# Groups 1 to 3 of a first feed-forward layer by Strassen's scheme too, and its successor's operands made a block ahead and kept on chip

## The chip, the cores and the metric

The kernel runs on one core of a Trainium2 chip. The metric is the device time of one execution in microseconds (us), lower is better. A core has five engines with a queue each: PE (TensorE, the matrix unit), DVE (VectorE), ACT (ScalarE), POOL (GpSimd) and SP (SyncE, which here only issues DMAs; ACT and POOL issue some too). Each engine works off its own list of instructions in order; semaphores make one wait for another.

## The reference, cut to what matters

Linear attention over 4 batches, 8 heads, 576 tokens and 64 columns a head gives x of 2304 tokens x 512 columns; then two feed-forward layers (FFN 1 and FFN 2) of 512 to 2048 to 512 columns.

```python
q_p, k_p = phi(q), phi(k)                     # random features, 128 per head
kv = np.einsum('bhsm,bhsd->bhmd', k_p, v)
x = (einsum(q_p, kv) / einsum(q_p, z))        # -> (2304, 512)
h = x @ w_in ; r = np.maximum(h, 0.0) ; y = (r * r) @ w_out          # FFN 1
h = y @ w2_in ; out = np.where(h > 0, h, exp(min(h, 0)) - 1) @ w2_out # FFN 2
```

All of it is float32. The FFN weights come as 64-bit floats and are turned into 32-bit ones on the chip.

## The kernel before, in words

**Limbs.** Each float32 operand of a matmul is held as two tiles, a high limb (names with h: xh, wh, gh) and a low limb (xl, wl, gl). A product is three matmuls: high x high, high x low, low x high. ACT makes high limbs (a copy), DVE low ones (`minus`, a subtraction).

**Blocks, tiles, groups.** The tokens lie in five blocks: blocks 0 to 3 have 512 tokens (one batch each), block 4, called B, has the 256 left over. The 2048 hidden columns are 16 tiles f of 128, in four groups g of four. Names carry these numbers: `st1_3_1` is the staged weight of layer 1 (FFN 2; FFN 1 is 0), tile 3, w_out (0 is w_in).

**FFN 1 before.** `steps` is the list of (group, block, tile): all five blocks for the four tiles of group 0, then of group 1, and so on. For each step `gemm1` (12 matmuls of 512 columns into one PSUM bank ph; ACT's relu r and square gh; DVE's gf and gl) is issued, then `gemm2` of the step two before (12 matmuls into py). After a group's four tiles DVE adds py into ya, the block's running sum. In group 0 blocks 0 to 2 go in halves of 256 tokens, the first 11 steps being woven into the attention; from step 11 on nothing else is left (`alone`). A `gemm1` also moves the decoding of weights ahead (`make`: ACT makes cm, DVE cv, of the staged tile st) and takes up to two entries of the list `later`.

**FFN 2 before.** `second` goes through tours, one for each group and block. A full block's tour is one of Strassen's products over the tiles: seven products (pa, pw, pb; 12 matmuls of 256 columns each) in place of eight, on sums of x pieces and on sums of weights (a, b, c, d; POOL makes them from each two tiles, cs and cd), and four chunks of the second matmul (12 matmuls of 512 columns). Copies us and vs and sums c21 and c22 join the products. Block B has no such scheme (pe, po: 24 matmuls each). x's operands of FFN 2 are made by `operands` at the end of each block of FFN 1 (POOL: eight subtractions of 256 columns; ACT and DVE split them) and stored to DRAM; each tour loads its own (`load_x`), only block 0's are kept on chip for the first.

**What sets the order.** The program is written out in order by hand. All tiles (x, limbs, weights, ya, temporaries) are pages of one pool of 93 (128x512 floats each): the next tile takes the page used longest ago, and its first writer waits for the last user of it. Eight PSUM banks go in the same way. Weights are fetched through three staging buffers, before the change by SP's queue, or POOL's for FFN 2 from tile 4 on.

## Time and profile before

| what | value |
|---|---|
| median of 3 runs | 938.9 us (938.43 to 938.97) |
| the profiled execution | 939.0 us, its span 937.2 us |
| granted TensorE clock, mean | 0.998 |
| PE busy | 921.5 us (98%) |
| DVE, ACT, POOL busy | 650.6, 498.7, 176.8 us |
| DMA | 131.25 MB, 140 GB/s over the span |

The span is the time from the first to the last instruction. PE's end times are modelled, so a busy PE need not be one at its peak.

### The profile page before, as it was taken

The numbers are of one execution on the slowest core, as the hardware profiler recorded it, in microseconds if no ns is written. First come the engines' busy times: TensorE is split into PE (matmuls) and PEld (weight loads), VectorE is DVE, ScalarE is ACT, GpSimd is POOL, SyncE is SP. The second block draws the span as 40 slices with busy tenths as digits, with TensorE's granted clock in tenths as the row PEclk, the third lists the DMA queues.
The fourth block names the chain that finished last, engine by engine and source line by source line (L and its number), as shares of the span: only waits on it lengthen the run. The fifth ranks groups of instructions, "written<-read, shape, count | busy, mean of one in ns | idle before, by whom it ended". The sixth has DMA issues, their size and how long they took to land.

```text
span 937.2 us, 17705 instructions
## 1 busy us (share of the span) xinstructions
PE 921.5 (98%) x6723; PEld 812.3 (87%) x6723; DVE 650.6 (69%) x1144; ACT 498.7 (53%) x1080; POOL 176.8 (19%) x299
## 2 busy tenths in 40 slices
PE   8998999999999999999999999999999999999997
PEld 7887889998888888888888888998898889988996
DVE  5989885753873378336789858996678667975553
ACT  6998975432432234223454446776377646665451
POOL 7666641000000000000133424400121002100000
PEclk9999999999999999999999999999999999999999
DMA  8554510110220023001254599785557756663632
GB/s 242 165 165 116 133 47 2 46 45 1 91 90 1 1 78 103 1 0 46 68 184 154 191 313 349 292 281 206 159 198 246 260 161 200 210 216 112 227 132 72
DMA packets 93749, 131.25 MB, mean 140 GB/s; under 512 B 30304, under 2 KB 48736, under 8 KB 93664
## 3 DMA queue, kind: packets, MB, share of 16 engines
q1 hardware_dynamic: 88240, 113.44, 37.2%
q0 software_dynamic: 4576, 16.26, 5.2%
q8 instruction: 53, 0.87, 0.4%
q10 hardware_dynamic: 848, 0.43, 0.2%
q14 instruction: 32, 0.26, 0.1%
HBM read 109.12 MB, written 20.97 MB: 139 GB/s over the span
## 4 chain that ended last, share of the span: by engine, by line
PE 87%; DVE 6%; ACT 5%; issue 1%; DMA 1%; SPq 0%; POOL 0%; ACTq 0%; DVEq 0%; POOLq 0%
PE py L688 21%; PE ph L498 21%; PE py L537 21%; PE pb L649 7%; PE pa L649 5%; PE pw L649 5%; PE po L769 1%; PE pe L769 1%; ACT ph0q L355 1%; DVE xl L76 1%; ACT ph2k L355 1%; ACT ph2q L355 1%; PE pn L419 1%; DVE cv L145 0%; ACT xh L453 0%
## 5 line engine op out<-in xcount | busy, mean ns | idle before, releaser
L509 ACT ACTIVATE r<-ph 128x512 f32<-128x512 f32 (+1 forms) x92 | 46.7, 507 | 229.3 <-PE ph L498 229.2
L513 DVE TENSOR_TENSOR gf<-r 128x512 f32<-128x512 f32 (+1 forms) x92 | 55.6, 605 | 130.3 <-ACT r L509 130.3
L498 PE MATMUL ph<-xh,wh 128*128 128x512 f32 (+1 forms) x368 | 127.5, 346 | 1.6 <-DVE xs L406 1.2
L537 PE MATMUL py<-gh,wh 128*128 128x512 f32 (+1 forms) x368 | 127.7, 347 | 0.0
L537 PE MATMUL py<-gl,wh 128*128 128x512 f32 (+1 forms) x368 | 126.9, 345 | 0.0
L537 PE MATMUL py<-gh,wl 128*128 128x512 f32 (+1 forms) x368 | 126.9, 345 | 0.0
L498 PE MATMUL ph<-xh,wl 128*128 128x512 f32 (+1 forms) x368 | 126.8, 345 | 0.0
L498 PE MATMUL ph<-xl,wh 128*128 128x512 f32 (+1 forms) x368 | 126.8, 345 | 0.0
L76 DVE TENSOR_TENSOR gl<-gf,gh 128x512 fp32r<-128x512 f32 (+1 forms) x164 | 106.2, 648 | 24.1 <-ACT gh L671 13.5
L688 PE MATMUL py<-wh,gh 128*128 128x512 f32 x288 | 113.6, 395 | 0.0
L688 PE MATMUL py<-wh,gl 128*128 128x512 f32 x288 | 113.6, 394 | 0.0
L688 PE MATMUL py<-wl,gh 128*128 128x512 f32 x288 | 113.4, 394 | 0.0
L662 DVE SCALAR_TENSOR_TENSOR r<-r,t 128x512 f32<-128x512 f32 x72 | 51.6, 716 | 67.0 <-ACT t L661 67.0
L498 PEld LDWEIGHTS ph<-xh,wh 128*128 128x128 f32 x368 | 69.2, 188 | 11.5 <-issue 1.3
L537 PEld LDWEIGHTS py<-gh,wh 128*128 128x128 f32 x368 | 69.2, 188 | 9.5
L537 PEld LDWEIGHTS py<-gh,wl 128*128 128x128 f32 x368 | 69.2, 188 | 9.2
L537 PEld LDWEIGHTS py<-gl,wh 128*128 128x128 f32 x368 | 69.2, 188 | 9.2
L498 PEld LDWEIGHTS ph<-xh,wl 128*128 128x128 f32 x368 | 69.2, 188 | 9.1
L498 PEld LDWEIGHTS ph<-xl,wh 128*128 128x128 f32 x368 | 69.2, 188 | 9.0
L671 ACT CAST gh<-gf 128x512 fp32r<-128x512 f32 x72 | 44.4, 617 | 48.8 <-DVE gf L663 48.7
L163 POOL TENSOR_TENSOR cs<-cv,cv 128x256 f32<-128x256 f32 x8 | 9.0, 1125 | 316.6 <-PE ph L498 307.2
L688 PEld LDWEIGHTS py<-wh,gl 128*128 128x128 f32 x288 | 54.1, 188 | 12.9
...
## 6 DMA issues: line engine op xcount, KB each, us to landing
...
```

The costliest lines, as they stand in the source:

```text
L76: eng.tensor_tensor(out=out, in0=whole, in1=hi.bitcast(F32), op=ALU.subtract)
L355: nc.scalar.activation(out=ph[:, i, :], in_=pp[:, i * M:(i + 1) * M], func=AF.Exp, bias=nb[:, 2 * i + g:2 * i + g + 1],)
L419: nc.tensor.matmul(pn[m, c * (D + 1):(c + 1) * (D + 1)], st[u]["qT"][h][:, c, m], st[b, "k", hp]["kv"][:, h, :], start=True, stop=True,)
L498: nc.tensor.matmul(ph[:, :n], wt[:, cs], x_part(xt, moe, i, c)[:, n0:n1], start=(m == 0), stop=(m == 3 * KD - 1))
L509: nc.scalar.activation(out=r, in_=ph[:, :n], func=AF.Relu)
L513: nc.vector.tensor_tensor(out=gf, in0=r, in1=r, op=ALU.mult)
L537: nc.tensor.matmul(y, w[:, ts], a, start=j == 0 and m == 0 and t % per == 0, stop=j == GF - 1 and m == 2, skip_group_check=per > 1,)
L649: nc.tensor.matmul(y[:, pr * HN:(pr + 1) * HN], wt[:, ws], x_view(tour, xn, l, v, e), start=first and pr == 0 and m == 0, stop=m == 5, ski ...
L662: nc.vector.scalar_tensor_tensor(out=r, in0=r, scalar=1.0, in1=t, op0=ALU.add, op1=ALU.mult)
L671: nc.scalar.copy(out=gh, in_=gf)
L688: nc.tensor.matmul(y_t[t], a[:, s0], w, start=first and pr == 0 and m == 0, stop=last and pr == 1 and m == 2,)
L769: nc.tensor.matmul(y[:, pr * HN:(pr + 1) * HN], wt[:, ws], x_view(tour, xn, 0, v, e), start=pr == 0 and m == 0, stop=m == 11, skip_group_c ...
```

## The change

FFN 1's groups 1 to 3 are taken out of `steps` and become tours of the same function that serves FFN 2 (`toured`): group 0 stays as it was. Their w_in tiles are summed on POOL as FFN 2's are (`summed_up`), which makes seven cast and split tiles per group in place of four. The operands of x for these tours are made in group 0, by `operands0`, from the limbs that attention left: POOL joins high and low limbs back (eight additions of 128x256 per full block, `xf`), and makes the terms t1 to t4 from them (four subtractions of 128x512); the splits follow (`operands0_limbs`). They stand in `later`, one entry per `gemm1` from step 11 on: block 0's sums at step 11, two idle entries, block B's, block 1's at step 15, block 0's four splits, block 2's sums at step 20, block B's split, block 1's four splits, block 3's sums at step 26, and the rest. The second matmul of FFN 1's tours has the weights stationary and moves 256 columns (96 matmuls per tour). FFN 2's operands are made right after a block's last sum in FFN 1, taken two at a time by `prepare(2)` at four places of a tour; all blocks' stay on chip for FFN 2's group 0. The w_out and w_in fetches of FFN 1 from tile 8 on and all of FFN 2's go by POOL's queue.

```diff
-    parts[2 * NF:] = sorted(parts[2 * NF:], key=lambda p: (p[1] // GF, p[2], p[1]))
+    parts[2 * GF:] = sorted(parts[2 * GF:], key=lambda p: (p[0], p[1] // GF, p[2], p[1]))
-            queue = nc.gpsimd if moe == 1 and f >= GF else nc.sync
+            queue = nc.gpsimd if moe == 1 or f >= 2 * GF else nc.sync
-    steps = [(0, g, o, j) for g in range(NG) for o in order(0, g) for j in range(GF)]
+    steps = [(o, j) for o in order(0, 0) for j in range(GF)]
+    tours = [(moe, g, k, o[0]) for moe in range(2) for g in range(NG) if moe or g for k, o in enumerate(order(moe, g))]
...
+    def prepare(n):
+        run(kept)
+        run(later, n)
+    def terms(moe, i, b):
+        tt = nc.gpsimd.tensor_tensor
+        if i == B:
+            d = page([W], f"d{moe}_{i}")
+            tt(out=d, in0=b[0, 1], in1=b[0, 0], op=ALU.subtract)
+            return [("d", d)]
+        ts = {name: page([W], f"{name}_{moe}_{i}") for name in TS}
+        tt(out=ts["t1"], in0=b[1, 0], in1=b[0, 0], op=ALU.subtract)
+        tt(out=ts["t2"], in0=b[1, 1], in1=ts["t1"], op=ALU.subtract)
+        tt(out=ts["t3"], in0=b[1, 1], in1=b[1, 0], op=ALU.subtract)
+        tt(out=ts["t4"], in0=b[0, 1], in1=ts["t2"], op=ALU.subtract)
+        return [(name, ts[name]) for name in ("t3", "t2", "t1", "t4")]
...
+        def joined():
+            b = {}
+            for l in range(1 if i == B else 2):
+                for k in range(2):
+                    b[l, k] = page([W], f"xf{i}_{l}_{k}")
+                    for e, (h, o) in enumerate(zip(piece(xh, l, k), piece(xl, l, k))):
+                        nc.gpsimd.tensor_tensor(
+                            out=b[l, k][:, e * HN:(e + 1) * HN], in0=h.bitcast(F32), in1=o.bitcast(F32), op=ALU.add
+                        )
+            found_t[i] = terms(0, i, b)
...
+                for e in range(2):
+                    ts = slice((2 * u + e) * P, (2 * u + e + 1) * P)
+                    for m, (a, w) in enumerate(((gh, oh), (gh, ol), (gl, oh))):
+                        nc.tensor.matmul(
+                            y_t[l, u][:, e * HN:(e + 1) * HN], w[:, ts], a[:, pr * HN:(pr + 1) * HN],
...
+        if moe == 0 and g == NG - 1 and l == (i < B):
+            operands1(i)
...
+            product(a, "a", 0, "b", True)
+            product(w, "c", 1, "t3", True)
+            nc.scalar.copy(out=b, in_=a)
+            nc.scalar.copy(out=vs, in_=w)
+            run(carried)
+            weights(tour)
+            earlier(0)
+            product(b, "c", 0, "t2")
+            nc.scalar.copy(out=us, in_=b)
+            product(a, "a", 1, "p")
+            act_a(tour, "11", a)
+            prepare(2)
+            earlier(1)
+            product(b, "b", 0, "t1")
+            nc.vector.tensor_tensor(out=c22, in0=b, in1=vs, op=ALU.add)
...
+                sums0 = [lambda i=i: operands0(i) for i in range(NB)]
+                limbs0 = [[lambda i=i, n=n: operands0_limbs(i, n) for n in range(4 if i < B else 1)] for i in range(NB)]
+                later.extend([sums0[0], idle, idle, sums0[B], sums0[1]] + limbs0[0] + [sums0[2]] + limbs0[B] + limbs0[1])
+                later.extend([sums0[3]] + limbs0[2] + limbs0[3])
```

**PE, block 1 of group 1.** Before, PE has these rows for the block's first tile, in `gemm1` and `gemm2` (each twelve long, of 512 columns):

```order
L498 MATMUL ph0_1_1_0_0_4503<-xh0_1_0_1254,wh0_4_0_3406 128x512 [waits DVE_49]
L498 MATMUL ph0_1_1_0_0_4503<-xl0_1_0_1255,wh0_4_0_3406 128x512
L498 MATMUL ph0_1_1_0_0_4503<-xh0_1_0_1254,wl0_4_0_3410 128x512
L537 MATMUL py0_1_1_0_0_4592<-gh0_1_1_0_0_4517,wh0_4_1_3451 128x512 [waits Activation_49]
L537 MATMUL py0_1_1_0_0_4592<-gh0_1_1_0_0_4517,wl0_4_1_3455 128x512
L537 MATMUL py0_1_1_0_0_4592<-gl0_1_1_0_0_4518,wh0_4_1_3451 128x512 [waits DVE_49]
```

After, the same block is a tour: the first of seven products (twelve such rows each, on operands xs loaded from DRAM) and the first of four chunks (24 such rows each):

```order
L662 MATMUL pa0_1_1_4874<-xsbh0_1_1_4500,wh0_4a_3451 128x256 [waits DMAHW2_49,Activation_49]
L662 MATMUL pa0_1_1_4874<-xsbl0_1_1_4501,wh0_4a_3451 128x256 [waits DMAHW3_49]
L662 MATMUL pa0_1_1_4874<-xsbh0_1_1_4500,wl0_4a_3504 128x256
L721 MATMUL py0_1_1_0_0_5180<-gh11_0_1_1_5001,wh0_4_1_3685 128x256 [waits PE_49,Activation_49]
L721 MATMUL py0_1_1_0_0_5180<-gh11_0_1_1_5001,wl0_4_1_3687 128x256
L721 MATMUL py0_1_1_0_0_5180<-gl11_0_1_1_5022,wh0_4_1_3685 128x256 [waits DVE_49]
```

So 96 matmuls of 512 columns become 84 + 96 of 256, and PE now waits for loads of x.

**POOL and ACT, steps 15 to 19 of group 0.** POOL has no row between the end of the attention and FFN 2's first weight sums before. After, this stands there for block 1 (behind four weight sums for tiles 4 and 5, five rows for block B and four weight sums for tiles 6 and 7):

```order
L620 TENSOR_TENSOR xf1_0_0_3622<-xh_1_0_1254,xl_1_0_1255 128x256
L620 TENSOR_TENSOR xf1_0_0_3622<-xh_1_1_1428,xl_1_1_1429 128x256
L620 TENSOR_TENSOR xf1_0_1_3625<-xh_1_2_1592,xl_1_2_1593 128x256 [waits DMAHW3_49,DMAHW2_49,Activation_49]
L620 TENSOR_TENSOR xf1_0_1_3625<-xh_1_3_1754,xl_1_3_1755 128x256
L620 TENSOR_TENSOR xf1_1_0_3628<-xh_1_0_1254,xl_1_0_1255 128x256 [waits Activation_49]
L620 TENSOR_TENSOR xf1_1_0_3628<-xh_1_1_1428,xl_1_1_1429 128x256
L620 TENSOR_TENSOR xf1_1_1_3631<-xh_1_2_1592,xl_1_2_1593 128x256
L620 TENSOR_TENSOR xf1_1_1_3631<-xh_1_3_1754,xl_1_3_1755 128x256
L594 TENSOR_TENSOR t1_0_1_3634<-xf1_1_0_3628,xf1_0_0_3622 128x512 [waits PE_49,Pool_49]
L595 TENSOR_TENSOR t2_0_1_3635<-xf1_1_1_3631,t1_0_1_3634 128x512 [waits PE_49,Pool_49]
L596 TENSOR_TENSOR t3_0_1_3636<-xf1_1_1_3631,xf1_1_0_3628 128x512 [waits Activation_49]
L597 TENSOR_TENSOR t4_0_1_3637<-xf1_0_1_3625,t2_0_1_3635 128x512 [waits PE_49,Pool_49]
```

ACT before, at steps 18 and 19 (third and fourth tile of block 2's first half):

```order
L509 ACTIVATE r0_0_2_0_2_3653<-ph0_0_2_0_2_3637 128x256 [waits PE_49]
L510 ACTIVATE gh0_0_2_0_2_3651<-r0_0_2_0_2_3653 128x256 [waits Activation_49]
L509 ACTIVATE r0_0_2_0_3_3688<-ph0_0_2_0_3_3672 128x256 [waits PE_49]
L510 ACTIVATE gh0_0_2_0_3_3686<-r0_0_2_0_3_3688 128x256 [waits Activation_49]
L509 ACTIVATE r0_0_2_256_0_3721<-ph0_0_2_256_0_3705 128x256 [waits PE_49]
```

ACT after, at the same place:

```order
L516 ACTIVATE r0_0_2_0_2_3773<-ph0_0_2_0_2_3757 128x256 [waits DMAHW0_49,DMAHW4_49,PE_49,Pool_49]
L517 ACTIVATE gh0_0_2_0_2_3771<-r0_0_2_0_2_3773 128x256 [waits Activation_49,Pool_49]
L576 CAST t1h0_0_3781<-t1_0_0_3390 128x512 [waits Pool_49]
L179 CAST wh0_4d_3801<-cd0_5_3479 128x512 [waits Pool_49]
L516 ACTIVATE r0_0_2_0_3_3819<-ph0_0_2_0_3_3803 128x256 [waits PE_49]
```

The relu, the square, the split and the weight cast now wait for POOL (their counts are reached with the seventh join of block 1, t1, t3 and t4 of block 1 in turn: each is the last user of the page that ACT's row writes next), and the next relu stands behind them.

**POOL, group 3, before the tour of block 3.** After, POOL's list has at this place (the weight sums of FFN 2's tiles 2 and 3 stand ahead):

```order
L594 TENSOR_TENSOR t1_1_1_8047<-ya0_1_256_0_3749,ya0_1_0_0_3500 128x512 [waits DMAHW3_49,DMAHW1_49,DVE_49]
L595 TENSOR_TENSOR t2_1_1_8048<-ya0_1_256_1_3751,t1_1_1_8047 128x512 [waits DVE_49,Pool_49]
L596 TENSOR_TENSOR t3_1_1_8049<-ya0_1_256_1_3751,ya0_1_256_0_3749 128x512 [waits DMAHW0_49,PE_49]
L597 TENSOR_TENSOR t4_1_1_8050<-ya0_1_0_1_3502,t2_1_1_8048 128x512 [waits DMAHW5_49,DMAHW6_49,Activation_49,Pool_49]
L121 DMA st1_3_1_8112<-in_moe2_w_out_dram 128x1024 [waits DMASW4_49]
```

And ACT's list, in the tour of block 3, is:

```order
L132 ACTIVATE cm1_1_1_8105<-st1_1_1_7797 128x512 [waits DMASW5_49,DVE_49,Pool_49]
L132 ACTIVATE cm1_2_1_8107<-st1_2_1_7802 128x512 [waits DMASW6_49,PE_49]
L132 ACTIVATE cm1_3_1_8114<-st1_3_1_8112 128x512 [waits DMASW7_49,PE_49]
L833 COPY us0_3_3_8057<-pb1_4467 128x512 [waits PE_49]
L676 ACTIVATE r11_0_3_3_8188<-pa0_3_3_8055 128x512 [waits PE_49]
```

This weight went by SP's queue before; now its fetch stands behind four sums that wait for DVE, and ACT's copy us stands behind its decoding.

## Rows read from the trace of the kernel before

**Rows 1.** The page's first lines: the span, and PE's busy time.

```profile
span 937.2 us, 17705 instructions
...
PE 921.5 (98%) x6723; PEld 812.3 (87%) x6723; DVE 650.6 (69%) x1144; ACT 498.7 (53%) x1080; POOL 176.8 (19%) x299
```

**Rows 2.** The page, shares of the chain of waits by engine.

```profile
PE 87%; DVE 6%; ACT 5%; issue 1%; DMA 1%; SPq 0%; POOL 0%; ACTq 0%; DVEq 0%; POOLq 0%
```

**Rows 3.** Busy time of each engine, clock, DMA share, GB/s, by stretch (groups 1, 3; FFN 2's 0).

```profile
245.00:345.40 100.40, 100.40 (x495) 84.14 (x494) 57.30 (x95) 32.91 (x58) 0.00 (x0) 1.00 0.16 49
...
445.80:546.20 100.40, 100.40 (x493) 83.90 (x491) 83.15 (x122) 46.52 (x87) 32.25 (x35) 1.00 0.45 156
...
560.00:655.50 95.50, 95.50 (x604) 86.00 (x602) 80.04 (x128) 66.91 (x120) 25.14 (x35) 1.00 0.80 285
```

**Rows 4.** PE's waits from 160 us to the end: total, times, longest us.

```profile
PE pb L649 <- DVE c L821: 0.8, 1, 0.8
```

**Rows 5.** The chain, FFN 1's group 0 in halves (start us, us, what).

```profile
174.56 1.42 PE ph L498 x12
...
201.53 1.41 PE py L537 x12
...
204.38 1.42 PE py L537 x12
```

**Rows 6.** The chain in a tour of FFN 2.

```profile
709.20 1.41 PE pa L649 x12
```

**Rows 7.** The chain in group 1 of FFN 1.

```profile
253.56 2.77 PE ph L498 x12
256.32 2.77 PE py L537 x12
```

**Rows 8.** Weight loads of `gemm1`, the page's groups (busy us, mean ns of one).

```profile
L498 PEld LDWEIGHTS ph<-xh,wh 128*128 128x128 f32 x368 | 69.2, 188 | 11.5 <-issue 1.3
```

**Rows 9.** ACT's timeline, in group 0 and in a tour (start us, us).

```profile
204.42 0.39 ACT L509 ACTIVATE r<-ph 128x256 f32<-128x256 f32 x1 [2.01 <-PE ph L498]
204.83 0.42 ACT L510 ACTIVATE gh<-r 128x256 fp32r<-128x256 f32 x1
...
701.31 0.62 ACT L671 CAST gh<-gf 128x512 fp32r<-128x512 f32 x1 [2.88 <-DVE gf L663]
```

**Rows 10.** POOL's timeline in group 3 (start us, us of the group, xcount).

```profile
461.78 0.75 POOL L163 TENSOR_TENSOR cs<-cv,cv 128x256 f32<-128x256 f32 x1 [307.20 <-PE ph L498]
...
463.43 1.07 POOL L165 TENSOR_TENSOR cs<-cv,cv 128x256 f32<-128x256 f32 x1
464.58 1.07 POOL L166 TENSOR_TENSOR cd<-cv,cs 128x256 f32<-128x256 f32 x1
...
476.25 1.81 POOL L606 TENSOR_TENSOR t<-ya,ya 128x256 f32<-128x256 f32 x2
...
490.97 1.36 POOL L592 TENSOR_TENSOR d<-ya,ya 128x512 f32<-128x512 f32 x1 [11.15 <-DVE ya L559]
```

**Rows 11.** DVE's timeline in group 0, last op of three of the decodings.

```profile
178.54 0.69 DVE L145 SCALAR_TENSOR_TENSOR cv<-cm,cv 128x512 uint32<-128x512 uint32 x1
...
182.09 0.69 DVE L145 SCALAR_TENSOR_TENSOR cv<-cm,cv 128x512 uint32<-128x512 uint32 x1
...
190.07 0.69 DVE L145 SCALAR_TENSOR_TENSOR cv<-cm,cv 128x512 uint32<-128x512 uint32 x1
```

**Rows 12.** The staging tile's operations, ns minimum/median/maximum; issue; us to landing.

```profile
L112 SPq DMA_DIRECT2D st<-in_moe_w_in_dram x20: 367/368/978, 5.0 to 457.6; - x20
...
L117 POOL DMA_DIRECT2D st<-in_moe_w_out_dram x12: 531/558/571, 585.6 to 799.3; - x12
...
DMA to landing us min/median/max: 3.4/4.0/10.2
```

**Rows 13.** DVE's timeline in a tour of FFN 2.

```profile
709.65 0.69 DVE L76 TENSOR_TENSOR gl<-gf,gh 128x512 fp32r<-128x512 f32 x1
710.25 1.28 DVE L701 TENSOR_TENSOR ya<-py,ya 128x512 f32<-128x512 f32 x2
```

More of the change, by code (lines that the diff above doesn't have):

```diff
@@ L187, in make_high @@
         p = parts[n]
[L188 removed]
+        if summed_up(p):
             return
@@ L613, in linear_attention_two_ffn_kernel @@
-    STEPS = (
-        ("a", "a", 0, "b", 0), ("w", "c", 1, "t3", 0), ("b", "c", 0, "t2", 0), ("a", "a", 1, "x", 0),
-        ("b", "b", 0, "t1", 0), ("w", "b", 1, "t4", 0), ("b", "d", 0, "x", 1),
-    )
-    tours = [(g, k, o[0]) for g in range(NG) for k, o in enumerate(order(1, g))]
-    full = [t for t in tours if t[2] < B]
-    x_t, bank, g2_t, sums, carried = {}, {}, {}, [], []
-    def load_x(tour, name):
-        g, k, i = tour
-        if (tour, name) in x_t:
-            return
-        ts = [page([W], f"xs{name}{s}{g}_{i}", F32R) for s in "hl"]
-        for v, t in enumerate(ts):
-            nc.sync.dma_start(out=t.bitcast(F32), in_=xd[i, name][:, v, :])
-        x_t[tour, name] = ts
@@ L630, in x_view @@
-    def x_view(tour, name, l, v, e):
-        if name == "x":
-            return x_t[tour, f"x{e}"][v][:, l * HN:(l + 1) * HN]
-        return x_t[tour, name][v][:, e * HN:(e + 1) * HN]
-    def product(tour, y, wn, wi, xn, l, first):
-        g, k, i = tour
-        for pr in range(2):
-            f = g * GF + 2 * pr
-            if wn == "d":
-                wh, wl = ws_t[g * GF, "d"]
-                w0 = pr * HP
-            else:
-                wh, wl = ws_t[f, wn]
-                w0 = wi * HP
+        if per == 2:
+            for t in range(KD // per):
+                ya = ya_t[i, n0 // HN, t] = page([W], f"ya0_{i}_{n0}_{t}")
+                nc.vector.tensor_copy(out=ya, in_=y_t[t])
+            return
@@ new lines, in linear_attention_two_ffn_kernel, with operands0_limbs, idle, load_x @@
+    found_t = {}
+    def operands0_limbs(i, n):
+        name, t = found_t[i][n]
+        split(0, i, name, t)
+    def idle():
+        pass
+    def load_x(tour, name):
+        moe, g, k, i = tour
+        if (moe, g, i, name) in x_t:
+            return
+        ts = [page([W], f"xs{name}{s}{moe}_{g}_{i}", F32R) for s in "hl"]
+        for v, t in enumerate(ts):
+            nc.sync.dma_start(out=t.bitcast(F32), in_=xd[moe, i, name][:, v, :])
+        x_t[moe, g, i, name] = ts
+    def times(tour, y, wn, w0, xn, first, last, fresh):
+        moe, g, k, i = tour
+        xs = x_t[moe, g, i, xn]
+        for pr in range(2):
+            if wn == "d":
+                wh, wl = ws_t[moe, g * GF, "d"]
+                c0 = pr * HN
+            else:
+                wh, wl = ws_t[moe, g * GF + 2 * pr, wn]
+                c0 = w0 * HN
@@ L703, in summed @@
+        if last:
+            sums.append(lambda: summed(tour, l))
+    def summed(tour, l):
+        moe, g, k, i = tour
+        for u in range(2):
+            key = (i, l, u)
+            if moe and g == 0:
+                ya_t[key] = page([W], f"ya1_{i}_{l}_{u}")
+                nc.vector.tensor_copy(out=ya_t[key], in_=y_t[l, u])
+            else:
+                nc.vector.tensor_tensor(out=ya_t[key], in0=y_t[l, u], in1=ya_t[key], op=ALU.add)
+            if moe == 0 or g < NG - 1:
                 continue
-            ya = ya_t.pop((i, t))
+            ya = ya_t.pop(key)
+            t = 2 * l + u
@@ L738, in weights, with toured @@
             make(lim, 2)
-    def second(before):
-        def run(fs):
-            while fs:
-                fs.pop(0)()
+    def toured(before):
         seeds = [psum(f"pb{n}") for n in range(2)]
-        wide = ws_t[0, "a"][0]
+        wide = ws_t[0, GF, "a"][0]
         for b in seeds:
@@ L792, in second, with product @@
             following = full[m + 1] if m + 1 < len(full) else None
[L794 to L799 removed]
+            def product(y, wn, w0, xn, fresh=False):
+                times(tour, y, wn, w0, xn, True, True, fresh)
+                if following and following[:2] != (1, 0):
+                    load_x(following, xn)
+            if n + 1 < len(tours) and tours[n + 1][3] == B and tours[n + 1][:2] != (1, 0):
                 for name in "uvd":
@@ L859, in moe_pieces @@
                 yield s
-        second([lambda s=s: gemm2(*steps[s]) for s in range(len(steps) - LOOK, len(steps))])
+        run(kept)
+        toured([lambda s=s: gemm2(*steps[s]) for s in range(len(steps) - LOOK, len(steps))])
     stages = (
```

329 lines of the change are left out of this document (145 added, 184 removed).

## The prediction

> **What bounds the kernel now.** First the page's engine shares: PE is busy 921.5 of 937.2 us [rows 1]. The chain of waits is PE for 87% of the span [rows 2]. The table by stage shows where PE has holes: in the stretches of the first FFN's groups and of the second's, PE's busy time equals the stretch (100.40 of 100.40 in groups 1 to 3 of the first, 95.50 of 95.50 in a group of the second), while DVE, ACT and the DMA engines have room [rows 3]. So in both FFNs the time is the number of matmul columns, and a change is worth the PE time that it removes, less every wait it puts before a matmul. PE's only recorded wait between 160 us and the end is 0.8 us, at the passage from the first FFN to the second [rows 4]. The profiled execution took 939.0 us, its span being 937.2; the median of the runs shown is 938.9, so I add my terms to 939.0.
>
> **Term 1, the products: -11.5.** Three prices are needed. A set of 12 matmuls of 256 columns takes 1.41 to 1.44 in group 0's halves [rows 5] and 1.41 in a tour [rows 6]; 22 such sets lie between 174.56 and 205.80, 1.42 each. A set of 12 of 512 columns takes 2.77 [rows 7]; from the period of a group, 100.40 = 32 such sets + 8 half sets of block B, it is (100.40 - 11.36) / 32 = 2.78. Before, a full block in groups 1 to 3 is eight sets of 512, 22.26. After, it is seven products (Strassen's) and 96 matmuls of 256 columns (eight half sets), 15 x 1.42 = 21.30. The gain is 0.96 a block, times 12 blocks 11.5. Block B keeps eight half sets: 0. Note how small this is: one of eight products is saved, in the first of two matmuls only.
>
> The second matmul now goes by 256 columns instead of 512, with twice as many weight loads. A weight load shows 188 ns [rows 8], longer than the 118 ns that a 256-column matmul takes in the rows, so loads overlap each other and the matmuls. Half sets in group 0 have the same shapes, weights loaded and all, and run at half the time of full ones [rows 5, 7], so I price this at nothing extra; the other end is rival (d). The Trainium skill speaks against the change here: its page "TensorE: Matmul & The Clock Gate", section "Back-to-back issue gap", says that weight load and matmul together set the spacing, and gives some 81 ns at 128 columns against 131 at 512, far from proportional; with 256 halfway, an estimate, fifteen half sets would cost 1.5 times eight full ones and the change would lose over 100 us. This trace shows 118 ns against 232, proportional, and the measurement decides.
>
> **Term 2, the old passage: -0.8.** The wait at 558 us [rows 4] arises when the last 128x512 blocks of the first FFN (four DVE additions at once) meet the first tour. After the change a tour follows a tour there, so it goes. A new passage lies between group 0 and group 1, after block B; there the copy into the product's bank stands on ACT behind a weight cast and a limb split: +0.3, an estimate of half an ACT cast of 0.62 [rows 9]; bounds 0 and 0.8, the old passage.
>
> **Term 3, POOL in group 0: +5.5.** POOL was idle for 307 us before 461.78 [rows 10]. Now, from the first step after attention (gemm1 step 11, at 174.56), it gets the weight sums of tiles 4 to 7 and the joins and sums of each block, and its pages come from the pool that relu's results use. The order shows what waits for it at step 18: relu's page comes free after the seventh of block 1's eight joins, gh's after t1 of block 1; then ACT has a split behind t3 and a weight cast behind t4, and step 19's relu stands behind both. So I run POOL's chain. It starts with cs0_5, which needs the second decoded part, ready at 182.09 + 0.69 = 182.8, and cs0_7 needs the fourth, 190.8 [rows 11] (the decoding keeps one part per step, only other parts). Chain: 4 ops for cs0_5, 4 joins and one 512-wide sum of block B, 4 ops for cs0_7, 8 joins, then t1, t2, t3, t4. PE wants gh of step 18 at 201.53 and gh of step 19 at 204.38 [rows 5].
> Prices. A 256-wide op takes 0.75 when DVE is idle, 1.07 when it is busy (with 1.15 from start to start where each waits for the one before), and 1.81 per pair, 0.9 each, where they don't wait; a 512-wide one 1.36 [rows 10], or 1.04 undisturbed if it loses the same 0.32.
> With 0.9 and 1.36: 182.8 + 8 x 0.9 + 1.36 + 4 x 0.9 + 8 x 0.9 = 202.2; t1 at 203.6, gh 0.42 later at 204.0 [rows 9], a stall of 2.5; t4 at 207.7, then cast 0.62, relu 0.39, square 0.42: 209.1, against 204.38 + 2.5 = 206.9, another 2.2. Together 4.7. The weight sums do wait for each other: 8 x 0.25 more gives 6.7. I take 5.5.
> Lower bound, all at 0.75 and 1.04: cs0_7 from 190.8, joins done 199.8, t1 200.8 (no stall), t4 204.0, gh of step 19 at 205.4: 1.0. Upper bound, all at 1.15 and 1.45: t1 208.7, stall 7.6, t4 213.1, then 2.5 more: 10.1.
> Whether DVE slows POOL so decides most of this term. The Trainium skill, "GPSIMD Engine Reference", section "Key points", says that GpSimd shares its SBUF interfaces with VectorE; 0.75 against 1.07 in this trace agrees. By undisturbed ops alone the sum would be 930.0, by disturbed ones 939.1.
> Later waits of this kind: relu of step 25 behind t4 of block 2. POOL needs 8 x 0.9 + 4 x 1.36 = 12.6 after block 1's t4 at 207.7, thus 220.3; the relu is due at 174.56 + 13 x 2.84 + 2.78 + 1.42 + 2.78 = 218.5 plus the 4.7 already lost, 223.2. Slack 2.9, price 0; without it, one for one.
>
> **Term 4, the queue of POOL in group 3: +2.0.** In the tour of group 3's block 3 the order has POOL's fetch of the last w_out part (st1_3_1) behind the four sums of block 1. ACT's cm1_3_1 needs that part and stands ahead of us0's copy, which PE awaits. The sums start with the tour: 4 x 1.36 to 1.45 = 5.4 to 5.8; issue 0.56; landing 4.0 in the median, 3.4 at least [rows 12]: landed 9.4 to 10.4 after the sums' start, which itself waits for DVE's two additions at the end of the tour before. In FFN 2 such additions start 1.05 after the next tour's first product and end 2.3 after it [rows 6, 13]; FFN 1's DVE is freer, so 0.1 to 2.3, and L, counted from the tour's start, is 9.5 to 12.7. us0 is due after two products, a chunk, two products and a chunk, 8 x 1.42 = 11.36; cm and the copy, at 0.62 each [rows 9], are done at L + 1.3. On DVE the third decoding stands before four lows, three decodings, gf, two limbs: thirteen ops at 0.60 from start to start [rows 13], so c22 is done at L + 7.8, for a use at 12 x 1.42 = 17.04. So the stall is L - 9.2: 0.3 to 3.5. I take 2.0, the middle; bounds 0 and 4 (a landing as late as the longest, 10.2 [rows 12], would make it 8, but it is one of 64).
>
> **Terms of nothing.** The operands of group 0 of FFN 2 stay on chip: loads go, but PE is full there with the DMA at 0.80 of its time [rows 3]; 0, since nobody waited for them. The loads of operands that FFN 1's tours now make (14 x 256 KB in 21 us, 175 GB/s) are no more than FFN 2's stretch carried at full PE, 285 GB/s [rows 3]; 0, and one for one where one lands late. The 12 stores of block 0 stand on SP ahead of the fetch for the fourth decoding: 12 x 0.37 to issue and 4.0 to land [rows 12] are 8.4, of the 10.8 between the last op of the first decoding, ended at 179.2, and that of the fourth, started at 190.07 [rows 11], which two more ops of DVE precede: 0, with little to spare, and beyond it one for one. DVE and ACT: in FFN 1 DVE is busy 57.30 of 100.40 [rows 3]; a tour adds two additions and three low limbs per block, some 15 per group: 0.
>
> **Sum.** 939.0 - 11.5 - 0.8 + 0.3 + 5.5 + 2.0 = 934.5.
>
> **The rivals.** (a) *The waits are hidden or short*, POOL being undisturbed and the fetch early: 927.0 + 1.0 + 0 to 1 = 928 to 929. For it: DVE idles two thirds of each step from 192 on before the change; against it: the limb splits and weight lows fill that. (b) *The gain is eaten*: both waits at their upper ends, 927.0 + 10.1 + 2 = 939.1, no change. For it: ops that wait for each other showed 1.15. (c) *Slower by POOL*: its joins read two pages and may run slower than any row. The chain has 20 ops of 256 and 5 of 512; where all take f times the upper prices, the stall grows by about 30 (f - 1). It passes 940.9, the bound for slower, at f = 1.06; at f = 1.25 stalls are 10.1 + 7.5 and relu of step 25 also waits, some 2: 949. Against it: the 512-wide sum of two pages took 1.36 in a stretch with DVE 83% busy [rows 3, 10]. (d) *Slower by weight loads*: the change loses from 22.26 / 15 = 1.484 a half set on. Were a half set in a tour bound by its loads one after the other, 12 x 0.188 = 2.26 [rows 8], a block would cost 33.8, 11.6 more than before: 12 x 11.6 = 139, 1078 with everything else at nothing. (The skill's rule above is of this kind.) Against it: every half set in the trace, 1.41 to 1.44. (e) *The change does nothing for PE*, since products and chunks are limited by something else in tours: excluded by FFN 2's period, 95.50 = 4 x (7 x 1.42 + 4 x 2.78) + 11.4, within 0.2.
>
> **How the numbers follow.** A difference of 0.2% (1.9 us) is about what this kernel's runs can tell from none. My forecast, stalls of 5 to 10: 0.48, of which 0.08 ends within 937.0 to 940.8. Hidden (a): 0.27. Eaten (b): 0.13, three fifths within 0.2%, the rest slower. Slower by POOL (c): 0.09; (d) and others: 0.03. Faster 0.67, same 0.16, slower 0.17. The range leaves out about 0.1 at the top and as much at the bottom: 927.5 to 940.5; the likeliest alone is 932 to 937.
>
> **What would show it.** Group 1, 2 and 3 should each take some 4 x 21.3 + 11.4 = 96.6 in place of 100.4. PE should have waits for ACT's gh near 202 to 212 that trace to POOL's xf1 and t; in group 3's last tour, for us0 or c22. POOL's joins at 0.9 and its sums at 1.36. If those waits are missing, the time is near 928; if 256-column sets in tours exceed 1.45, or waits show in more than these two places, I am wrong on the high side.

## The result and the profile after

The change made the kernel slower: 950.67 us in the median (949.48 to 950.98, 4 runs) against 938.81 (938.43 to 938.97, 4 runs), a ratio of 1.0125, 95% interval [1.0107, 1.0142]. The profiled execution's span is 949.1 us against 937.2 [rows 1], so 11.9 us are to be found.

The page of the kernel after, with the busy time of each engine, beside [rows 1]:

```profile
span 949.1 us, 20503 instructions
...
PE 917.3 (97%) x7731; PEld 856.1 (90%) x7731; DVE 703.4 (74%) x1170; ACT 528.9 (56%) x1126; POOL 261.9 (28%) x370
```

PE is busy less (917.3 against 921.5), POOL 85 us more, DVE 53 us more. PE's work has shrunk; the loss lies in waits and in a lower clock. PE's waits from 150 us on (total, times, longest), beside the single 0.8 of [rows 4]:

```profile
PE py L540 <- DVE gl L76: 9.2, 5, 3.2
PE pb L662 <- ACT pb L827: 3.1, 1, 3.1
PE pb L662 <- DVE c L839: 2.0, 3, 1.0
PE pb L662 <- ACT us L833: 1.7, 1, 1.7
```

By stretch (busy time of PE, PEld, DVE, ACT and POOL, each with its instructions in brackets; granted clock, DMA share, GB/s), beside [rows 3]:

```profile
173.00:200.00 27.00, 24.69 (x204) 23.84 (x203) 23.95 (x37) 11.30 (x26) 13.68 (x15) 1.00 0.56 176
200.00:225.00 25.00, 18.05 (x121) 17.35 (x122) 24.36 (x25) 10.23 (x23) 24.84 (x22) 0.86 0.36 132
...
245.00:265.00 20.00, 19.50 (x138) 18.05 (x136) 13.32 (x29) 7.01 (x15) 1.73 (x2) 1.00 0.97 337
265.00:285.00 20.00, 17.24 (x130) 17.04 (x131) 14.62 (x24) 11.29 (x20) 1.50 (x2) 0.91 0.99 359
...
349.00:446.00 97.00, 97.00 (x824) 97.00 (x823) 60.57 (x99) 39.61 (x67) 11.94 (x16) 1.00 0.62 214
446.00:543.00 97.00, 94.00 (x791) 93.38 (x790) 67.26 (x100) 43.88 (x77) 26.73 (x24) 1.00 0.65 234
543.00:560.00 17.00, 16.35 (x138) 16.14 (x137) 17.00 (x24) 9.87 (x18) 5.60 (x4) 1.00 0.50 188
```

Between 173 and 225 us PE lacks 9.3 us and DVE has none left (24.36 of 25.00); the granted clock is 0.86 of full in the second of these stretches. The next holes are at 245 to 285 (3.3 us, the DMA engines full) and at 446 to 560 (3.7 us). Group 2, at 349 to 446, is full.

To put the whole into an account I take marks that both traces have. PE's first matmul of step 11 starts at 174.40 before and 175.51 after, and its first of group 1 at 244.97 and 259.63 (timelines of PE). After that the first product of block B stands in the chain once for each group:

```profile
278.34 2.83 PE pe L662 x24
...
374.68 2.82 PE pe L662 x24
...
471.07 2.83 PE pe L662 x24
...
572.33 2.84 PE pe L662 x24
```

The last of these lies at 560.40 in the trace before. Between them 96.34, 96.39 and 101.26 us; a group took 100.40 [rows 3].

| part | us |
|---|---|
| end of the attention (174.40 to 175.51) | +1.1 |
| group 0 (70.57 to 84.12) | +13.5 |
| first tour (18.7 from 259.63 to block B's product, for 9 half sets of 1.42, the 0.45 of the seeds and 0.1 between) | +5.3 |
| group 3 (101.26 in place of 96.36) | +4.9 |
| the rest: products, old passage | -12.9 |
| sum, of 11.9 | +11.9 |

The last line but one is what is left over; terms 1 and 2 with the new passage's 0.3 taken out had said -12.3. Group 0 is the largest part. DVE's timeline in it (start, us):

```profile
203.34 1.22 DVE L76 TENSOR_TENSOR t3l<-t,t3h 128x512 fp32r<-128x512 f32 x1
204.48 1.23 DVE L76 TENSOR_TENSOR wl_6a<-cv,wh_6a 128x512 fp32r<-128x512 f32 x1
205.64 0.95 DVE L520 TENSOR_TENSOR gf<-r 128x256 f32<-128x256 f32 x1
206.69 0.76 DVE L76 TENSOR_TENSOR gl<-gf,gh 128x256 fp32r<-128x256 f32 x1
...
209.08 1.27 DVE L551 COPY ya<-py 128x512 f32<-128x512 f32 x2
```

In the trace before, a 128x256 gf or gl takes 0.42 or 0.43 in these steps and a 128x512 low limb 0.69 (as in [rows 13]):

```profile
204.83 0.43 DVE L513 TENSOR_TENSOR gf<-r 128x256 f32<-128x256 f32 x1 [1.90 <-ACT r L509]
205.36 0.42 DVE L76 TENSOR_TENSOR gl<-gf,gh 128x256 fp32r<-128x256 f32 x1
```

Here they take 0.95, 0.76 and 1.22 to 1.23. The copy of ya, which reads PSUM, takes 0.64 as ever. POOL works without a pause at that time (a group of eight joins, then the sums):

```profile
198.82 8.36 POOL L620 TENSOR_TENSOR xf<-xh,xl 128x256 f32<-128x256 f32 x8
207.14 1.48 POOL L594 TENSOR_TENSOR t<-xf,xf 128x512 f32<-128x512 f32 x1
208.69 1.63 POOL L595 TENSOR_TENSOR t<-xf,t 128x512 f32<-128x512 f32 x1
210.28 1.80 POOL L596 TENSOR_TENSOR t<-xf,xf 128x512 f32<-128x512 f32 x1
212.04 1.44 POOL L597 TENSOR_TENSOR t<-xf,t 128x512 f32<-128x512 f32 x1
```

What PE does meanwhile, first when gl comes late, then some 3 us later:

```profile
202.33 0.39 PE L540 MATMUL py<-gl,wh 128*128 128x256 f32 x1 [2.94 <-DVE gl L76]
202.57 0.28 PE L540 MATMUL py<-gh,wh 128*128 128x256 f32 x1
...
205.21 0.41 PE L507 MATMUL ph<-xh,wl 128*128 128x256 f32 x1
205.42 0.41 PE L507 MATMUL ph<-xh,wh 128*128 128x256 f32 x1
```

After 2.94 us without work the matmuls go on at 0.12 from start to start, but soon at 0.21: the granted clock has gone to its lower level (1.2 instead of 2.4 GHz) for a while. By the spacing of the matmuls this costs group 0 some 3 of its 13.5 us; the rest are the waits, 9.2 us by the record, and about 0.2 us more for each, until PE is back at its pace.

### The profile page after: what moved, and what is told of

Read it like the earlier page. It is cut to its first block, busy times and chain, and to the rows that moved or that the text cites. A ratio compares the mean times of both kernels' runs of the same rounds, so it can differ in the third digit from the quotient of the medians.

```text
span 949.1 us, 20503 instructions
## 1 busy us (share of the span) xinstructions
PE 917.3 (97%) x7731; PEld 856.1 (90%) x7731; DVE 703.4 (74%) x1170; ACT 528.9 (56%) x1126; POOL 261.9 (28%) x370
## 4 chain that ended last, share of the span: by engine, by line
PE 67%; DMA 4%; DVE 3%; issue 1%; SPq 1%; POOL 1%; ACT 1%; DVEq 0%; POOLq 0%; ACTq 0%
PE py L713 21%; PE py L721 14%; PE pb L662 12%; PE pa L662 8%; PE pw L662 7%; PE po L662 2%; PE pe L662 2%; DMA st<-in_moe_w_out_dram 1%; PE ph L507 1%; DMA xd10q<-qh 1%; DMA xst4h<-xd00t 1%; SPq L571 1%; DMA xsdl<-xd04d 0%; DMA xst3h<-xd00t 0%; PE py L540 0%
## 5 line engine op out<-in xcount | busy, mean ns | idle before, releaser
L721 PE MATMUL py<-gh,wl 128*128 128x256 f32 x432 | 121.3, 281 | 0.0
L721 PE MATMUL py<-gh,wh 128*128 128x256 f32 x432 | 121.3, 281 | 0.0
L721 PE MATMUL py<-gl,wh 128*128 128x256 f32 x432 | 121.2, 281 | 0.0
L737 DVE TENSOR_TENSOR ya<-py,ya 128x512 f32<-128x512 f32 x108 | 70.7, 684 | 23.1 <-PE py L721 12.8
L116 POOL DMA_DIRECT2D st<-in_moe_w_in_dram x24 | 18.3, 766 | 204.2 <-DVE cv L140 164.2
L678 DVE TENSOR_TENSOR gf<-r 128x512 f32<-128x512 f32 x54 | 37.9, 713 | 41.3 <-ACT r L676 40.9
L713 PEld LDWEIGHTS py<-wl,gh 128*128 128x128 f32 x288 | 54.1, 188 | 10.0
L713 PEld LDWEIGHTS py<-wh,gh 128*128 128x128 f32 x288 | 54.1, 188 | 9.9
L140 DVE SCALAR_TENSOR_TENSOR cv<-st,cv 128x512 uint32<-128x512 uint32 x64 | 48.4, 756 | 2.2
L540 PE MATMUL py<-gl,wh 128*128 128x256 f32 (+1 forms) x128 | 38.9, 304 | 9.3 <-DVE gl L76 9.2
```

What stands on the lines that cost most here:

```text
L116: queue.dma_start(out=t.rearrange("p (c f) t -> p c (f t)", c=KD), in_=w[:, f * 2 * P:(f + 1) * 2 * P].rearrange("(c p) f -> p c f", p=P),)
L140: nc.vector.scalar_tensor_tensor(out=t, in0=lo, scalar=29, in1=t, op0=ALU.logical_shift_right, op1=ALU.bitwise_or)
L540: nc.tensor.matmul(y, w[:, ts], a, start=j == 0 and m == 0 and t % per == 0, stop=j == GF - 1 and m == 2, skip_group_check=per > 1,)
L678: nc.vector.tensor_tensor(out=gf, in0=r, in1=r, op=ALU.mult)
L713: nc.tensor.matmul(y_t[l, u], a[:, s0], w, start=first and pr == 0 and m == 0, stop=last and pr == 1 and m == 2,)
L721: nc.tensor.matmul(y_t[l, u][:, e * HN:(e + 1) * HN], w[:, ts], a[:, pr * HN:(pr + 1) * HN], start=first and pr == 0 and m == 0 and e == 0 ...
```

## The experiments

Each kernel is timed against the kernel before on the same chip; ratios are to that. Three theories stood at the start: P, that POOL's two-input operations slow DVE's, DVE is then full, and PE waits for gl; Q, that the splits the change adds are too many for DVE; R, the forecast's, that pages held by POOL hold up ACT.

**e1, the changed kernel without FFN 1's joins and sums.**

```diff
-            b = {}
...
-                        nc.gpsimd.tensor_tensor(
-                            out=b[l, k][:, e * HN:(e + 1) * HN], in0=h.bitcast(F32), in1=o.bitcast(F32), op=ALU.add
-                        )
-            found_t[i] = terms(0, i, b)
+            names = ("d",) if i == B else ("t3", "t2", "t1", "t4")
+            found_t[i] = [(name, flat(xh[i, c]).bitcast(F32)) for c, name in enumerate(names)]
```

> The changed kernel without FFN 1's joins and sums of x on POOL (the splits take pages of x in their place, so the operands are other numbers; ACT's, DVE's and the DMAs' work is as before). Theory P (POOL's two-input operations slow DVE's, which is then full in group 0, and PE waits for its gl): DVE's 128x512 subtractions fall from 1.22 back to 0.69 between 185 and 225 us, the five waits of PE for gl (9.2 us) go, and with them some 13 us: 936 to 939. Theory Q (the splits and weight lows that the change adds to DVE are too many by themselves): the waits for gl stay, 946 to 950. Theory R (pages that POOL holds): as P in time, but DVE's durations are no cause, and runs e2 and e3 tell.

Measured: 936.38 us, ratio 0.9966 [0.9952, 0.9980]. It leaves the sums out, so its splits work on other numbers, but the instructions of ACT, DVE and PE are the change's. The waits for gl are one of 1.1 us, and block B's first product starts at 261.18 instead of 278.34. Q falls: the same splits are there, their low limbs take 0.69, and DVE copes. Without its sums the kernel would beat the one before, although it still loses 5.5 us in group 3 (101.8 from block B to block B). The first tour, too, takes 14.5 us instead of 18.7, at a DMA share of 0.94 to 1.04: full DMA engines alone do not make it wait.

**e2 and e8, POOL's work beside the kernel before.** Nobody reads these results, so no data dependence can hold anything up. Both have 91 pages in the pool instead of 93, two being spare.

```diff
+    spare = [const.tile([P, W], F32, name=f"spare{u}") for u in range(2)]
+    def beside(i):
...
+        tt = nc.gpsimd.tensor_tensor
+        for k in range(8 if i < B else 4):
+            l, c = (k // 4, k % 4) if i < B else (0, k)
+            h, o = (x_part(d, 0, i, c)[:, l * 256:(l + 1) * 256].bitcast(F32) for d in (xh, xl))
+            tt(out=spare[k % 4 // 2][:, k % 2 * 256:(k % 2 + 1) * 256], in0=h, in1=o, op=ALU.add)
+        for k in range(4 if i < B else 1):
+            tt(out=spare[0], in0=spare[0], in1=spare[1], op=ALU.subtract)
...
+            if s in (11, 14, 15, 20, 26):
+                beside({11: 0, 14: B, 15: 1, 20: 2, 26: 3}[s])
```

> The kernel before, with the same joins and sums on POOL at the same steps of group 0, into two spare tiles that nobody reads (the page pool is 91 instead of 93). No one waits for POOL. Theory P: DVE's two-input operations of 128x512 take about 1.2 instead of 0.69 while POOL runs; DVE, 57% busy here before, fills up, and PE loses 0 to 6 us: 939 to 945. Theories Q and R: DVE's durations stay at 0.69 and the time within 0.5 of 938.8.

Measured: 952.98 us, ratio 1.0149 [1.0127, 1.0171], above the expected range, and by itself more than the whole change costs. The same with one-input operations, two for each of those with two:

> As the run with the sums beside the kernel before, but every two-input operation on POOL replaced by two operations with one input (a product by 1). If it is two inputs on POOL that slow DVE, DVE's 128x512 subtractions stay at 0.69 and the time at 938 to 941; if any POOL work beside DVE does, they go to 1.2 again, and the time to 945 to 955.

Measured: 940.27 us, ratio 1.0008 [0.9998, 1.0019]. DVE's groups between 174 and 226 us (busy us, mean ns of one), in the run with two inputs:

```profile
L524 DVE TENSOR_TENSOR gf<-r 128x256 f32<-128x256 f32 x13 | 11.9, 913 | 4.0 <-ACT r L520 4.0
...
L76 DVE TENSOR_TENSOR wl<-cv,wh 128x512 fp32r<-128x512 f32 x4 | 6.0, 1492 | 0.0
...
L565 DVE COPY ya<-py 128x256 f32<-128x256 f32 x12 | 4.2, 408 | 0.0
```

and in the run with one input, where POOL was busy even longer (49.4 of 52 us against 44.6):

```profile
L526 DVE TENSOR_TENSOR gf<-r 128x256 f32<-128x256 f32 x14 | 7.5, 538 | 8.7 <-ACT r L522 8.7
...
L76 DVE TENSOR_TENSOR wl<-cv,wh 128x512 fp32r<-128x512 f32 x4 | 2.9, 730 | 0.0
...
L567 DVE COPY ya<-py 128x256 f32<-128x256 f32 x17 | 6.0, 414 | 0.0
```

1492 ns against 730 for the same low limb, 913 against 538 for gf, and no difference for the copies that read PSUM. So it is POOL's two-input operations beside DVE's operations on SBUF. One-input operations do some of the same (gf took 0.42 before), but PE loses only 1.0 us to them. Nor is it the two pages, which e8 lacks as well. R is not needed: here nothing waits for POOL.

**e3, FFN 1's joins and sums on DVE**, `nc.vector` for `nc.gpsimd` in `joined` and `terms`.

> The changed kernel with FFN 1's joins and sums of x on DVE instead of POOL (the same operands). Theory P: a block costs DVE 8 x 0.36 + 4 x 0.6 = 5.3 us, about what 14 us of POOL take from it at 1.2 for 0.69 (6 us), and it's done sooner: no worse, 942 to 950, with DVE's 128x512 subtractions at 0.69. Theory Q or R: DVE gets 23 us more work where it is already full, so 20 us more: 960 to 972.

Measured: 948.99 us, ratio 1.0100 [1.0085, 1.0115]. DVE's low limbs are back at 0.69, the waits for gl are 11.1 us. What the sums cost DVE stands in its busy time (third pair) from 150 us to group 1's first matmul, in e1, in the change and here:

```profile
150.00:246.65 96.65, 95.47 (x791) 89.97 (x791) 66.31 (x135) 43.04 (x100) 8.62 (x12) 1.00 0.56 189
150.00:259.63 109.63, 100.38 (x813) 93.90 (x807) 91.04 (x138) 44.29 (x103) 69.09 (x65) 0.97 0.45 152
150.00:261.36 111.36, 100.24 (x792) 94.03 (x791) 88.71 (x188) 43.10 (x100) 8.19 (x12) 0.94 0.49 166
```

Beside POOL's sums DVE is busy 24.7 us longer with nearly the same operations (three more); the 53 sums on DVE itself make it 22.4 us. So the work costs DVE in its own queue about what it cost as contention, which is thus measured from both sides. In time the sums on DVE are the dearer ones in group 0 (86.9 us from step 11 on, against 84.1), since DVE does a block's twelve in a row and PE waits once for 7.1 us; the first tour makes up for it (14.5 against 18.7).

**e4, blocks 2 and 3 later.**

```diff
-                later.extend([sums0[0], idle, idle, sums0[B], sums0[1]] + limbs0[0] + [sums0[2]] + limbs0[B] + limbs0[1])
-                later.extend([sums0[3]] + limbs0[2] + limbs0[3])
+                later.extend([sums0[0], idle, idle, idle, idle] + limbs0[0] + [sums0[B], idle, idle, idle, sums0[1]])
+                later.extend([idle] * 3 + limbs0[B] + limbs0[1] + [idle] * 3)
+                late.extend([sums0[2], idle] + limbs0[2] + [sums0[3], idle] + limbs0[3])
```

`late` is appended to `later` when the tours begin.

> The changed kernel with the sums and splits of blocks 2 and 3 taken out of group 0 and made in the tours of group 1, and more room between those of blocks 0, B and 1. Theory P: in group 0 POOL runs 28 us less beside DVE, the waits for gl fall from 9.2 to 2 to 5 us; the loads of the first tour meet fewer stores: 938 to 944. Theory Q: as many splits fewer in group 0 (8 of 17), about the same. A rival to both: the waits only move into group 1's tours, 948 to 952.

Measured: 953.06 us, ratio 1.0144 [1.0122, 1.0166]: the rival holds, a little above its range. Group 0's waits for gl fall from 9.2 to 3.3, but the tours of group 1 now wait, once 5.6 us for a weight's low limb and once 4.3 for gl, at a clock of 0.82 between 265 and 285 us.

**e5 and e6, one or two fetches on another queue** (the first + is e5's, the second e6's).

```diff
-            queue = nc.gpsimd if moe == 1 or f >= 2 * GF else nc.sync
+            queue = nc.gpsimd if (moe == 1 or f >= 2 * GF) and p != (1, GF - 1, 1) else nc.sync
+            queue = nc.gpsimd if moe == 1 or f >= 2 * GF or (f, o) in ((6, 1), (7, 1)) else nc.sync
```

> The changed kernel with one fetch, that of the last w_out part of FFN 2's group 0, on SP's queue instead of POOL's, where it stood behind block 1's sums. Theory: this fetch causes the 3.65 us for which PE idles in the tours of group 3 (and the lower clock after them), 4.9 in all: group 3 falls from 101.3 to 96.4, time 945 to 947. Rival: POOL's sums slow DVE there and c22 is late anyway: 949 to 951.

Measured: 948.90 us, ratio 1.0091 [1.0071, 1.0110]. The wait for ACT's us (1.7) is gone and group 3 takes 99.7 instead of 101.3; the waits for c22 stay (2.4). So the fetch behind the sums is about a third of term 4's 4.9 us, not all. (The interval of the whole time still touches the change's own; the 1.6 us are read in group 3, which takes 99.6 to 99.7 us in e10 and e12 as well.)

> The changed kernel with the fetches of the last two w_out parts of group 1 on POOL's queue, idle there, instead of SP's behind the loads of x. Theory: at the passage from group 0 to group 1 ACT's decoding waits for this fetch because it stands in SP's queue; PE's wait of 3.1 us for ACT's copy goes: 946 to 948.5. Rival: the DMA engines, 0.97 to 0.99 busy there, are the limit, and it lands late by either queue: 949.5 to 951.5.

Measured: 952.72 us, ratio 1.0137 [1.0110, 1.0164], above both ranges. The passage does what was expected: PE's wait for ACT's copy falls from 3.1 to 0.6, the first tour from 18.7 to 14.6 us. But the waits for gl rise from 9.2 to 16.0, 8.8 of it in one, and DVE's timeline has its reason:

```profile
212.19 7.33 DVE L76 TENSOR_TENSOR gl<-gf,gh 128x256 fp32r<-128x256 f32 x1
```

while POOL, after the issue of the moved fetch, goes through eight joins at 0.69 each, against 1.04 in the change:

```profile
211.77 0.75 POOL L121 DMA_DIRECT2D st<-in_moe_w_out_dram  x1
212.54 5.49 POOL L620 TENSOR_TENSOR xf<-xh,xl 128x256 f32<-128x256 f32 x8
```

One operation of 0.42 took 7.33 us: here POOL did not slow DVE but seems to have kept it out, until the joins and the sum behind them (its end 219.24) were done. Only one such row stands in the profiles of this study.

**e7, Strassen only from FFN 1's group 2 on.** Group 1 goes through `gemm1` and `gemm2` as before, the x operands are made from step 30 to the end of group 1; the last fetch goes by SP as in e5.

```diff
...
-    steps = [(o, j) for o in order(0, 0) for j in range(GF)]
+    steps = [(g, o, j) for g in range(2) for o in order(0, g) for j in range(GF)]
-    tours = [(moe, g, k, o[0]) for moe in range(2) for g in range(NG) if moe or g for k, o in enumerate(order(moe, g))]
+    tours = [(moe, g, k, o[0]) for moe in range(2) for g in range(NG) if moe or g > 1 for k, o in enumerate(order(moe, g))]
...
```

> Strassen in FFN 1's groups 2 and 3 only; group 1 goes as in the kernel before, and the joins, sums and splits of x are spread over the last steps of group 0 and over group 1, where DVE was 57% busy; the last fetch as in the run before last. Theory P: DVE has 43 us of slack in group 1, so POOL's 56 us of two-input work cost it some 24 us and PE nothing: 938.8 - 2 x 4.04 - 0.8 + 0 to 3 = 930 to 933. Rival: PE is so close behind DVE step by step that it waits anyway: 935 to 942.

Measured: 944.75 us, ratio 1.0054 [1.0035, 1.0074]: better than the change by 6 us, but past the range of the rival too. PE waits 3.9 us for gl and 3.0 for ya.

**e9, only block 0's operands kept on chip** for FFN 2's group 0, the others loaded as for its other groups:

```diff
-        if moe:
+        if moe and i == 0:
             x_t[1, 0, i, name] = h, l
...
```

> The changed kernel, but only block 0's operands are kept on chip for FFN 2's group 0, as before; the others are loaded back from DRAM. All theories: nobody waits for these loads, 950 to 951.5; if keeping them was worth anything, more.

Measured: 948.80 us (947.61 to 952.16), ratio 1.0101 [1.0074, 1.0128], below the expected range, with an interval that overlaps the change's own. FFN 2's group 0, block B to block B, takes 95.6 us, and 95.5 in the change: keeping the operands bought nothing that can be measured. The profiled execution is the shorter by its first tour, 15.4 us instead of 18.7, though up to there its instructions are the change's:

```profile
PE pb L662 <- ACT pb L827: 1.4, 1, 1.4
...
257.53 6.71 DMA st<-in_moe_w_out_dram
```

The fetch that ACT waits for lands 1.7 us sooner than in the change's profile, PE waits 1.4 us instead of 3.1, and its clock stays up. So the cost of the first tour varies by 3 us from one execution to another.

**e10, e11, e12: less for DVE in `gemm1`.** e10 is the changed kernel, e11 the one from group 2 on, e12 the one with sums on DVE, each with the last fetch by SP and with

```diff
+        nc.scalar.activation(out=gf, in_=r, func=AF.Square)
...
-        nc.vector.tensor_tensor(out=gf, in0=r, in1=r, op=ALU.mult)
```

> The changed kernel with gf = r x r in group 0 made by ACT (10 of 25 us busy there) instead of DVE, and the last fetch by SP as in an earlier run. Theory P (DVE, slowed by POOL's two-input work, is what PE waits for in group 0): DVE is rid of 0.95 us a step, so most of the 9.2 us of waits for gl and of the 3 us of lower clock behind them go: 937 to 941. If PE waits there for POOL's pages, the time stays at 947 to 949.

> The kernel with Strassen from FFN 1's group 2 on, with gf by ACT in groups 0 and 1. Theory P: its waits for DVE (3.9 for gl, 3.0 for ya) shrink by half or more: 936 to 942, from 944.8.

> As the run with the square by ACT, but with the joins and sums of x on DVE. Theory P: DVE at its own speed has 23 us more work in group 0 and 11 us less: waits for gl of 3 to 6 us, 938 to 943. It tells which of the two, POOL's contention or DVE's own work, is dearer: the better of the two kernels is less than 3 us better.

Measured: 941.32 (ratio 1.0015 [1.0005, 1.0026]), 940.62 (1.0013 [1.0003, 1.0024]) and 944.37 us (1.0049 [1.0033, 1.0065]). e10 misses its range by 0.3. With one operation of DVE less per step it is 9 us faster than the change; by the profiles 2.0 of them lie before step 11 (173.52 against 175.51), 2.2 in group 0, 3.8 in the first tour (14.9 us, though the two fetches stand on SP's queue as before; e9 is 3.3 shorter there with the change's own instructions) and 1.6 in group 3, from the fetch. Its waits for gl are 5.4 us, and 2.6 for ACT's gh have come, which the change doesn't have. The longer of these two follows POOL's sum t1, as term 3 said:

```profile
206.71 0.42 ACT L517 ACTIVATE gh<-r 128x256 fp32r<-128x256 f32 x1 [1.98 <-POOL t L594]
```

e12 misses its range by 1.4: its waits for gl stay at 10.6 us, as DVE does the sums in a few bursts (the longest wait is 7.1).

**e13 and e14, versions.** In e11 PE stood 4.5 us without a matmul from 278 us on, waiting for ya's additions, which stood on DVE behind block B's split, which waited for ACT and for POOL's sum. e13 sets the splits further behind their sums than e11 does (its lines are those with a minus); e14 moves FFN 2's sums in group 3 to DVE too.

```diff
-                for i in (0, B, 1, 2, 3):
-                    later.extend([sums0[i], idle] + limbs0[i] if i < B else [sums0[i]] + limbs0[i])
+                later.extend([sums0[0], idle, idle] + limbs0[0] + [sums0[B], sums0[1], idle] + limbs0[B] + [idle] + limbs0[1])
+                for i in (2, 3):
+                    later.extend([sums0[i], idle, idle] + limbs0[i])
...
-        tt = nc.gpsimd.tensor_tensor
+        tt = nc.vector.tensor_tensor if moe else nc.gpsimd.tensor_tensor
```

> The kernel with Strassen from group 2 on and the square by ACT, with the splits set two or three steps behind their sums, so that DVE no longer stands at block B's split behind POOL while PE waits for the additions of ya (4.7 us without a matmul, and a lower clock after it). Theory P with queue order: 934 to 937, faster than the kernel before. If the waits only move on, 938 to 941.

> The same with FFN 2's sums in group 3 on DVE (four operations of 0.6 a block in place of POOL's four of 1.4 that slow DVE). If POOL's contention makes c22 late there (3.2 us of waits for c), they shrink: 1 to 3 us less than the run beside it. If it is the order on DVE's queue, the time stays within 0.5.

Measured: 939.98 us, ratio 1.0008 [0.9996, 1.0020], and 938.03 us, ratio 0.9980 [0.9969, 0.9992], against 939.53 for the kernel before in the same rounds: in e13 the waits only moved on, e14 gains what was expected. PE's waits in e13:

```profile
PE pb L671 <- DVE c L848: 3.1, 4, 1.0
PE py L730 <- DVE wl L76: 2.0, 1, 2.0
PE ph L507 <- DVE ya L555: 0.4, 1, 0.4
```

and in e14:

```profile
PE py L730 <- DVE wl L76: 2.0, 1, 2.0
PE pb L671 <- DVE c L848: 1.0, 2, 0.8
```

The wait for ya is down to 0.4; a wait of 2.0 for a weight's low limb has come in group 2's first tour, and the runs scatter (937.2 to 943.2, and 936.2 to 941.5). With the sums on DVE the waits for c22 fall from 3.1 to 1.0 and PE's busy time between 446 and 543 us rises from 94.65 to 96.69: those waits were POOL's contention as well. Group 3, block B to block B, takes 97.4 us instead of 99.6. (The two profiled executions are equal within 0.1 us, as e14's comes to its first tour 1.8 us later; that the kernel is faster is in the runs.) e14 is the one complete version that is faster than both kernels, by 0.2% of the kernel before, which is little more than its interval.

## Why the prediction was wrong

**Term 1 was right.** Groups 1 and 2 (block B to block B) take 96.34 and 96.39 us against a forecast of 96.6, a half set 1.41 to 1.43 in tours. Twice as many weight loads cost nothing, and rival (d) did not happen. The sustained spacing that the Trainium skill's page "TensorE: Matmul & The Clock Gate" gives in "Back-to-back issue gap" is not borne out (118 ns against 232 for twice the columns).

**Term 2** took the passage at +0.3; the first tour lost 5.3 (3.1 in a wait for ACT's copy, most of the rest at a lower clock, 0.91 in that stretch). The chain there goes through loads and a fetch:

```profile
252.14 6.23 DMA xst4h<-xd00t
...
258.39 7.52 DMA st<-in_moe_w_out_dram
...
265.93 0.03 ACT cm L132
...
267.10 0.49 ACT pb L827
...
267.63 2.18 PE pb L662 x12
```

ACT's decoding cm waited for a fetch of w_out that stood in SP's queue behind the loads of x. With the fetches elsewhere (e6), or DVE sooner (e1, e10), the tour loses 1.2 to 1.6. But e9 loses only 2.1 with the change's own order. So the term's size was missed by the order on SP's queue, which it did not price; how much of the gain in e1, e6 and e10 is theirs, and how much belongs to the execution, is not shown.

**Term 3 failed**, in its mechanism and not only in size. It asked only who waits for POOL, and put 5.5 us on PE's waits for ACT's gh. Group 0 took 13.5 us more, and PE's five waits there, 9.2 us, are for DVE's gl. The waits of ACT that it forecast are there (1.9 us for t1 at step 18; 3.0 for t3 and 0.8 for t4 at step 19), but PE, already late because of gl, takes gh without a wait; only where DVE has less to do (e10) does PE wait for it, 2.6 us. Its chain of POOL came out at its upper end (t4 done at 213.5, forecast at most 213.1), in part by luck: eight joins took 8.36 us (1.04 each) and the sums 1.44 to 1.80, but 2.5 us are a wait of POOL itself for DVE's decoding.

The contention which the term named as the reason why POOL is slower (0.75 against 1.07) was counted on POOL alone. It holds both ways: DVE's operations grew to 1.75 times and more. (The Trainium skill's sentence in "GPSIMD Engine Reference", "Key points", names contention with DVE's instructions that have two SBUF inputs, and could have been read so; this trace agrees, with 1.22 for 0.69.) And no term had DVE's load in group 0: the 57% were for the tours, and rival (a) says only that DVE idles two thirds of each step there and that splits and weight lows fill that. In the trace before that is so:

```profile
200.00:225.00 25.00, 25.00 (x168) 22.97 (x168) 10.32 (x23) 6.92 (x14) 0.00 (x0) 1.00 0.01 1
```

In the same stretch DVE is busy 17.6 us with splits and weight lows (e1) and 24.36 with POOL's sums beside them. e2 shows the contention with no dependence at all, e8 that most of it needs two inputs, e1 that without the sums it is gone. Nor did the sum hold anything for the clock, which fell after two of these waits.

**Term 4** was right in its place and near in the size of what it named: the fetch behind the sums costs about 1.6 (e5) of the 2.0 forecast. But group 3 lost 4.9, above the term's upper bound of 4: the waits for c22 are POOL's sums slowing DVE (e14), the cause missed in term 3. The lower clock has no part in it (1.00 in both stretches of group 3); each wait costs PE about 0.3 us more from matmul to matmul than the record calls idle.

**Terms of nothing:** keeping operands on chip is nothing (e9), and DVE's work in tours was nothing in groups 1 and 2, as forecast. In group 3, where POOL's sums come to it, it was not: an average over a group does not say what DVE has left in the steps where work is added.

Of the rivals, (c) had the right sign and engine, its time of 949 close to the measured one, but by luck: it reached it by slower joins and pages. No rival had DVE as the one that is late, and the range ended at 940.5 for that reason. (Rival (b) speaks of both waits at their upper ends but adds 2 for term 4, whose upper end was 4; by that it stands at 941.1.)

What stays open: how the 1.1 us at the end of the attention come about (step 11 starts at 174.4 and 174.5 where POOL makes no joins of x, in e1 and e3, at 175.1 to 175.5 in the change, e5 and e9, but at 174.1 in e6), why the runs of e13 and e14 scatter by 5 us, and when POOL shares with DVE and when it keeps it out (e6).
